# First layer's differences spread over four points, attention's loads and groups moved, two sums of the second layer behind other products, the last block's sums in another order with one on POOL

## The chip, the core and the metric

The kernel runs on one core of a Trainium2 chip. Its engines work side by side and meet by semaphores: TensorE (PE, with its weight loads PEld), VectorE (DVE), ScalarE (ACT), GpSimd (POOL) and SyncE (SP), whose queue issues all the DMAs here. Each engine takes its instructions in the order of the program. The metric is the time of one execution on the device in microseconds, the median of several runs.

## What is computed

Attention in chunks of 32 queries, each over 8 memory slots and a window of 56 keys, and on its result two feed-forward layers, all in fp32:

```
scores = scale * q_c @ k_full.T ; a = softmax(scores) ; out[:, :, chunk] = a @ v_full
x = out.transpose(0, 2, 1, 3).reshape(B * S, H * D)          # 3072 x 512
h = x @ w_in ;  g = relu(h) ** 2            ; x = g @ w_out  # layer 0, d_ff 2048
h = x @ w_in ;  g = h * tanh(log1p(exp(h))) ; x = g @ w_out  # layer 1
```

## The kernel before

The tokens are cut into three blocks (`sb`) of 1024, the hidden dimension into eight parts of 256 (`NQ`). One step is one part of one block of one layer; there are 48, steps 0 to 23 for layer 0 (blocks 0 to 2) and 24 to 47 for layer 1 (blocks 3 to 5 in the code's count). Every fp32 operand is held as a rounded high part and a rest, and a product is made of three matmul passes.

The first matmul of a layer uses a scheme of seven products in place of eight (`PRODUCTS`: P1 to P7, on blocks B11, B21, B12, B22 of x and on the differences T1 = B12 - B11, T2 = B22 - T1, T3 = B22 - B12, T4 = B21 - T2). DVE adds the products up through u1, u2, u3 to c22, c21, c12; P7 may start only when u2 has been read out of its bank, P4 only after u3, P3 only after c22. `gate` applies the activation, and `split_g` (a cast on ACT, a subtraction on POOL) makes the two parts of g. The second matmul belongs to the step before: in layer 0 it is eight `unit`s of six matmuls, unit n for output half t = n // 4 and quarter d = n % 4, summed into `y` by DVE (for the first part of a block it is ACT that copies into y, L547); in layer 1 it is seven `product2`s of six matmuls (`PRODUCTS2`), summed by DVE into tiles m (L558), again by an ACT copy for the first part (L581). When a block is done, the m tiles are combined by the seven additions of `SUMS`, and four of them are stored as the block's output.

`step` writes out the order by hand. Between groups of matmuls it calls `rest()`, which counts points 0 to 14 of a step: it issues the waiting stores (`flush`, in the order of `later`), then the weight loads of that point (`stream_w`), then what was put there by `at(step, point, ...)`. In steps 1 to 24 the points come after P1 (0), P6 (1), P5 (2), units 0 and 1 (3, 4), P2 (5), P7 (6), units 2 to 4 (7 to 9), P4 (10), P3 (11), units 5 to 7 (12 to 14). In steps 25 to 47 they come after P1 (0), P6 (1), product 0 (2), P5 (3), product 1 (4), P2 (5), product 2 (6), P7 (7), products 3 and 4 (8, 9), P4 (10), P3 (11), products 5 and 6 (12, 13).

Put beside the matmuls in this way are the decoding and splitting of the weights (`plan_w`: rebias A/a, decode D/d, sums S/s, round R/r, split L/l), the attention of blocks 1 and 2 (`plan_attention`, groups p = 4 to 7 in steps 0 to 6 and p = 8 to 11 from step 9 on: scores, softmax, exps, normalize, transposes, values, `copy_x`, `sums_x` on POOL, `store_x`), the load and split of the next block's x (`load_x` at points 0 to 6, `split_x` from point 4 of the block's last step), and in layer 1 the loads ahead for the next block. Attention's later groups keep q and p in the tile xt0, k in at0, v and the staged result in at1; the next block's xt use the same tiles.

The differences of a finished block of layer 0 are made in `sums_y`, called at the end of steps 8, 16 and 24: three stores of y, four DVE subtractions into tiles of their own, four stores. The tiles y0 and y1 are taken anew for each block, and in layer 1 for four of the m tiles; a new tile waits for all readers of the old one. In the last step (47) and after it, DVE makes the remaining sums and the additions of the last four units (L603, `last_unit`).

## Time and profile before

| | us |
|---|---|
| median of 3 runs (1128.75, 1129.05, 1133.09) | 1129.05 |
| the profiled execution | 1126.08 |
| its span, first to last instruction | 1124.2 |
| PE / DVE / ACT / POOL busy in it | 1061.5 / 898.6 / 561.6 / 430.5 |
| DMA, mean share of 16 engines | 0.81 |

A busy share is a mean over stages that differ: steps 0 to 15 hold attention and the decoding of the weights, steps 16 to 24 the rest of layer 0, steps 25 to 47 layer 1. PE's matmuls are pipelined, so its busy time holds overlaps; the time from the first matmul of P1 in one step to that in the next is what is called a step's time here. The granted clock is given as a share of 2.4 GHz: 1.00 is the upper of two levels, 0.50 the lower.

### The profile page before, as it was taken

How to read it: one execution, taken by the hardware profiler on the slowest of the kernel's cores; microseconds unless marked ns; L12 is line 12 of the kernel's file. 1: busy time of each engine (PE TensorE's matmuls, PEld its weight loads, DVE VectorE, ACT ScalarE, POOL GpSimd, SP SyncE). 2: the span in 40 equal slices, each digit the busy share in tenths (PEclk: the TensorE clock that was granted, in tenths of full speed). 3: DMA queues.
4: the chain of work that ended last, by engine and by line, in shares of the span. 5: the costliest groups of instructions: out<-in, count | busy, mean ns of one | idle time of the engine just before them, and what ended most of it. 6: DMA issues, size and time to landing. Idle time of an engine off the chain costs nothing.

```text
span 1124.2 us, 19766 instructions
## 1 busy us (share of the span) xinstructions
PE 1061.5 (94%) x7478; PEld 872.3 (78%) x7478; DVE 898.6 (80%) x1170; ACT 561.6 (50%) x879; POOL 430.5 (38%) x327
## 2 busy tenths in 40 slices
PE   5779999897799999999999999999999999999997
PEld 5758787785677887888888878888878888778885
DVE  5686889969756766578999767988888888978888
ACT  2458555546544554647656555443354444444331
POOL 1215233232223333223322244546454554545552
PEclk9998999999989999999999999999999999999999
DMA  9556867777989898969999968989979889797441
GB/s 354 216 186 269 308 228 275 259 265 268 369 316 319 306 333 298 336 237 381 374 345 328 361 225 292 316 312 324 401 247 319 308 307 371 272 315 227 158 155 75
DMA packets 192125, 324.94 MB, mean 289 GB/s; under 512 B 13344, under 2 KB 151072, under 8 KB 188192
## 3 DMA queue, kind: packets, MB, share of 16 engines
q1 hardware_dynamic: 192032, 323.69, 80.9%
q8 instruction: 60, 0.98, 0.3%
q14 instruction: 33, 0.27, 0.1%
HBM read 231.62 MB, written 92.01 MB: 288 GB/s over the span
## 4 chain that ended last, share of the span: by engine, by line
PE 65%; DVE 14%; DMA 6%; issue 4%; ACT 3%; POOL 1%; SPq 0%; DVEq 0%; ACTq 0%; POOLq 0%
PE banks L480 29%; PE banks L535 16%; PE banks L570 15%; DVE m L558 3%; PE banks L416 1%; PE banks L346 1%; DVE r L521 1%; DMA w_d<-hi 1%; DMA w2s<-w_d 1%; DVE y L549 1%; DMA w1s<-w_d 1%; DVE ty L628 1%; DVE val L157 1%; DVE val L158 1%; DVE val L154 1%
## 5 line engine op out<-in xcount | busy, mean ns | idle before, releaser
L480 PE MATMUL banks<-x,w1s 128*128 128x512 f32 x2016 | 502.2, 396 | 19.1 <-DVE u L763 7.3
L494 POOL TENSOR_TENSOR g<-r,g 128x512 fp32r<-128x512 f32 x206 | 289.6, 1412 | 523.1 <-ACT g L493 434.6
L480 PEld LDWEIGHTS banks<-x,w1s 128*128 128x128 f32 x2016 | 382.3, 191 | 104.4 <-DVE u L763 9.0
L535 PE MATMUL banks<-g,w2s 128*128 128x512 f32 x1152 | 279.7, 394 | 6.9 <-DVE y L549 6.7
L535 PEld LDWEIGHTS banks<-g,w2s 128*128 128x128 f32 x1152 | 216.7, 190 | 55.7 <-DVE y L549 8.4
L570 PE MATMUL banks<-g,w2s 128*128 128x512 f32 x966 | 239.0, 390 | 1.2 <-DVE m L558 0.6
L570 PEld LDWEIGHTS banks<-g,w2s 128*128 128x128 f32 x966 | 180.6, 188 | 41.9 <-DVE m L558 2.3
L558 DVE TENSOR_TENSOR m<-banks,m 128x1024 f32<-128x1024 f32 x144 | 173.3, 1218 | 30.5 <-PE banks L570 27.5
L493 ACT CAST g<-r 128x512 fp32r<-128x512 f32 x206 | 127.0, 621 | 31.0 <-DVE r L521 23.7
L549 DVE TENSOR_TENSOR y<-banks,y 128x512 f32<-128x512 f32 x168 | 111.4, 682 | 25.7 <-PE banks L535 25.4
L494 POOL TENSOR_TENSOR g<-more,g 128x512 fp32r<-128x512 f32 x55 | 81.8, 1492 | 77.8 <-ACT g L493 63.2
L499 ACT ACTIVATE r<-r 128x512 f32<-128x512 f32 x72 | 45.4, 631 | 69.5 <-DVE r L771 46.1
L503 ACT ACTIVATE r<-r 128x512 f32<-128x512 f32 x48 | 30.3, 632 | 75.8 <-DVE r L765 38.4
L213 ACT CAST hi<-val 128x1024 fp32r<-128x1024 f32 (+1 forms) x32 | 30.4, 951 | 71.4 <-DVE val L158 42.3
L500 ACT ACTIVATE r<-r 128x512 f32<-128x512 f32 x96 | 60.7, 633 | 3.1
L154 DVE TENSOR_SCALAR val<-val 128x512 f32<-128x512 f32 x64 | 36.7, 573 | 24.4 <-ACT val L147 24.4
L346 PE MATMUL banks<-k,q 64*32 64x64 f32 x1536 | 39.4, 255 | 16.8 <-DMA k<-k_dram 10.1
L346 PEld LDWEIGHTS banks<-k,q 64*32 64x32 f32 x1536 | 33.4, 125 | 21.5 <-issue 18.2
L158 DVE SCALAR_TENSOR_TENSOR val<-raw,val 128x512 uint32<-128x512 uint32 x64 | 47.3, 738 | 2.2
L735 ACT COPY u<-banks 128x512 f32<-128x512 f32 x48 | 27.9, 581 | 41.1 <-PE banks L480 41.0
L386 POOL TENSOR_TENSOR p<-p,sum 128x512 f32<-128x512 f32 x22 | 25.6, 1186 | 57.8 <-DVE sum L383 23.3
L416 PE MATMUL banks<-pt,v 64*64 64x32 f32 x1536 | 35.1, 249 | 11.3 <-ACT pt L404 9.8
(72 smaller groups left out, 991.4 us busy)
## 6 DMA issues: line engine op xcount, KB each, us to landing
w1s<-w_d SPq DMA_DIRECT2D x280, 256.0 KB, 5.5
w2s<-w_d SPq DMA_DIRECT2D x229, 256.0 KB, 5.4
raw<-w_dram SPq DMA_DIRECT2D x64, 512.0 KB, 5.1
w_d<-w1s SPq DMA_DIRECT2D x8, 1792.0 KB, 7.1
x<-xs_d SPq DMA_DIRECT2D x14, 1024.0 KB, 10.7
k<-k_dram SPq DMA_DIRECT2D x24, 512.0 KB, 7.3
v<-v_dram SPq DMA_DIRECT2D x24, 512.0 KB, 8.7
xt<-xt_d SPq DMA_DIRECT2D x21, 512.0 KB, 7.3
```

The source lines that it names most:

```text
L154: nc.vector.tensor_scalar(out=val, in0=val, scalar1=LIMIT, scalar2=-LIMIT * NEGATIVE, op0=ALU.min, op1=ALU.max)
L158: nc.vector.scalar_tensor_tensor(out=vb, in0=low, scalar=29, in1=vb, op0=ALU.logical_shift_right, op1=ALU.bitwise_or)
L346: nc.tensor.matmul(out=s4[32 * c:32 * c + 32, j, hp, :], lhsT=q_t[p][r0:r0 + 64, j, hp, 32 * c:32 * c + 32], rhs=k_t[p][r0:r0 + 64, j, hp, ...
L416: nc.tensor.matmul(out=x_ps[par][64 * h2:64 * h2 + 64, o:o + 32], lhsT=v_t[p][j][r0:r0 + 64, h2, a, c, :], rhs=pt_t[p][r0:r0 + 64, h2, j, ...
L480: nc.tensor.matmul(out=ps, lhsT=w[:, a, f:f + 128], rhs=x[:, xi, c, kk, :], start=start and i == 0, stop=stop and i == len(order) - 1, ski ...
L493: nc.scalar.copy(out=g[:, 0], in_=r)
L494: nc.gpsimd.tensor_tensor(out=g[:, 1], in0=r, in1=g[:, 0].bitcast(FP32), op=ALU.subtract)
L500: nc.scalar.activation(out=r, in_=r, func=ACTF.Square)
L535: nc.tensor.matmul(out=ps, lhsT=w[:, a, blk(f), d % 2 * 128:d % 2 * 128 + 128], rhs=g_t[s, (f, t)][:, c, :], start=i == 0, stop=i == len(o ...
L549: nc.vector.tensor_tensor(out=y, in0=ps, in1=y, op=ALU.add)
L558: engine.tensor_tensor(out=to, in0=in0, in1=in1, op=ALU.add)
L570: nc.tensor.matmul(out=bank(first + d), lhsT=w[:, a, 128 * d:128 * d + 128], rhs=g[:, c, :], start=i == 0, stop=i == 2)
```

## The change

The tile y of a block is used again for the next one instead of being taken anew, and so are the two tiles that hold four of the m tiles. `sums_y` is replaced by `plan_sums`: the stores of B11 and B21 come at points 5 and 9 of the block's last units, the first difference at point 13, the store of B22 and the second difference at point 0 of the next step, the fourth at point 1 and the third at point 3; the fourth is written over B21, the third over B12, and the first two share the tile at1. In attention, the load of v moves from 5 to 8 points behind the group's start; the groups of block 1 follow each other by 24 points instead of 25, those of block 2 start at point 10 of step 8 with a period of 20 instead of point 8 of step 9 with 19, with q and k of the first loaded at points 0 and 1 of step 8. In the weights' plan for steps 8 to 14, r and l move by one point. In layer 1, the sum of B22 and T2 moves from behind product B21 to behind T3, and that of B21 and B11 from behind T3 to behind T1. In the last step the sum of B21 and B11 goes to POOL behind T3, and that of T3 and T2 moves from behind T1 to behind T2.

```diff
--- before.py
+++ after.py
@@ -449,7 +449,7 @@
         nc.vector.tensor_tensor(out=to[1], in0=st, in1=to[0].bitcast(FP32), op=ALU.subtract)
 
 
-    g_t, y_t, m_t = {}, {}, {}
+    g_t, y_t, m_t, m_both = {}, {}, {}, {}
     rings = {"g": 0, "r": 0, "u": 0}
     more = {}
 
@@ -541,7 +541,7 @@
             )
         rest()
         if j == 0 and d == 0:
-            y_t[sb, t] = pool.tile([128, KD, NB], FP32, tag=f"y{t}", name="y")
+            y_t[sb, t] = y_t[sb - 1, t] if sb else pool.tile([128, KD, NB], FP32, tag=f"y{t}", name="y")
         y = y_t[sb, t][:, d]
         if j == 0:
             nc.scalar.copy(out=y, in_=ps)
@@ -576,17 +576,21 @@
             if n < 3:
                 m_t[sb, blk] = pool.tile([128, 2, NB], FP32, tag=spare(sb + 1, n), name="m")
             elif n % 2:
-                both = pool.tile([128, 2, 2, NB], FP32, tag=f"y{n // 5}", name="m")
+                if sb == NSB:
+                    both = pool.tile([128, 2, 2, NB], FP32, tag=f"y{n // 5}", name="m")
+                else:
+                    both = m_both[n]
+                m_both[n] = both
                 m_t[sb, blk], m_t[sb, PRODUCTS2[n + 1][1]] = both[:, 0], both[:, 1]
             nc.scalar.copy(out=m_t[sb, blk], in_=ps)
             return
         m = m_t[sb, blk]
         add(m, ps, m)
 
-    def combine(sb, to, other, store=False):
+    def combine(sb, to, other, store=False, engine=nc.vector):
 
         m = {b: m_t[sb, b] for _, b in PRODUCTS2}
-        add(m[to], m[to], m[other])
+        add(m[to], m[to], m[other], engine)
         if store and (to, other) in SUMS[3:]:
             store_y(sb, *OUTPUTS[to], m[to])
 
@@ -612,22 +616,6 @@
         store_y(sb, i, t, m)
         flush()
 
-    def sums_y(sb):
-        d = xt_d[1][sb]
-        y0, y1 = y_t[sb, 0], y_t[sb, 1]
-        b11, b21, b12, b22 = (i.rearrange("p k s -> p (k s)") for i in (y0[:, 0:2], y0[:, 2:4], y1[:, 0:2], y1[:, 2:4]))
-        nc.sync.dma_start(out=d[:, B11], in_=b11)
-        nc.sync.dma_start(out=d[:, B21], in_=b21)
-        nc.sync.dma_start(out=d[:, B22], in_=b22)
-        if sb < NSB - 1:
-            both = [pool.tile([128, 2, 2 * NB], FP32, tag=f"at{n}", name="ty") for n in range(2)]
-            t = [both[n // 2][:, n % 2] for n in range(4)]
-        else:
-            t = [pool.tile([128, 2 * NB], FP32, tag=("xt0", "xt1", "xt2", "at1")[n], name="ty") for n in range(4)]
-        for n, (t1, t2) in enumerate(((b12, b11), (b22, t[0]), (b22, b12), (b21, t[1]))):
-            nc.vector.tensor_tensor(out=t[n], in0=t1, in1=t2, op=ALU.subtract)
-            later(d[:, T1 + n], t[n])
-
 
     beside = {}
 
@@ -642,7 +630,8 @@
             1: lambda: softmax(p, 0),
             2: lambda: softmax(p, 1),
             3: lambda: (exps(p, 0), exps(p, 1), load_k(p + 1) if (p + 1) % PSB else None),
-            5: lambda: (normalize(p), load_v(p) if p > PSB else None),
+            5: lambda: normalize(p),
+            8: lambda: load_v(p) if p > PSB else None,
             12: lambda: transpose_p(p),
             13: lambda: (copy_pt(p), load_q(p + 1) if (p + 1) % PSB else None),
             16: lambda: values(p),
@@ -651,6 +640,46 @@
             22: lambda: store_x(p),
         }.items():
             at(s, i + n, work)
+
+    def plan_sums(sb):
+
+
+        d = xt_d[1][sb]
+        t = {}
+
+        def blocks():
+            y0, y1 = y_t[sb, 0], y_t[sb, 1]
+            return [i.rearrange("p k s -> p (k s)") for i in (y0[:, 0:2], y0[:, 2:4], y1[:, 0:2], y1[:, 2:4])]
+
+        def minus(n, to, in0, in1):
+            nc.vector.tensor_tensor(out=to, in0=in0, in1=in1, op=ALU.subtract)
+            later(d[:, n], to)
+
+        def first():
+            b11, _, b12, _ = blocks()
+            t["both"] = pool.tile([128, 2, 2 * NB], FP32, tag="at1", name="ty")
+            minus(T1, t["both"][:, 0], b12, b11)
+
+        def second():
+            b22 = blocks()[3]
+            later(d[:, B22], b22)
+            minus(T2, t["both"][:, 1], b22, t["both"][:, 0])
+
+        def fourth():
+            b21 = blocks()[1]
+            minus(T4, b21, b21, t["both"][:, 1])
+
+        def third():
+            _, _, b12, b22 = blocks()
+            minus(T3, b12, b22, b12)
+
+        s = (sb + 1) * NQ
+        at(s, 5, lambda: later(d[:, B11], blocks()[0]))
+        at(s, 9, lambda: later(d[:, B21], blocks()[1]))
+        at(s, 13, first)
+        at(s + 1, 0, second)
+        at(s + 1, 1, fourth)
+        at(s + 1, 3, third)
 
     def plan_w(s, i, e, order, round_, split, val):
 
@@ -718,13 +747,13 @@
             _, sb, j = where(s - 1)
             blk = PRODUCTS2[i][1]
             if s == STEPS - 1:
-                for n in {T2: (0,), T1: (1, 2, 3), T4: (4, 6, 5)}.get(blk, ()):
-                    combine(sb, *SUMS[n])
+                for n in {T3: (6,), T2: (0, 1), T1: (2, 3), T4: (4, 5)}.get(blk, ()):
+                    combine(sb, *SUMS[n], engine=nc.gpsimd if n == 6 else nc.vector)
             elif j == NQ - 1:
                 for n in {T2: (0,), T1: (1,)}.get(blk, ()):
                     combine(sb, *SUMS[n])
             elif sb > NSB and j == 0:
-                for n in {B11: (3,), B22: (4,), B21: (5,), T3: (6,)}.get(blk, ()):
+                for n in {B11: (3,), B22: (4,), T3: (5,), T1: (6,)}.get(blk, ()):
                     combine(sb - 1, *SUMS[n], store=True)
 
         if live:
@@ -786,8 +815,6 @@
             for w in beside.pop((s, i), []):
                 w()
         flush()
-        if prev and where(s - 1)[0] == 0 and where(s - 1)[2] == NQ - 1:
-            sums_y(where(s - 1)[1])
 
     with tc.manual_schedule():
         nc.scalar.preload_act_table_set("natural_log_exp_and_others")
@@ -868,7 +895,7 @@
         seconds = [e for e in order_w if e[0]]
         for n, e in enumerate(seconds):
             if n < NQ - 1:
-                plan_w(NQ + n, 0, e, "Aa|D|d|RS|s|L||||r|l", lambda e, i: round_w2(e, i, "xt2"), split_w2, "val")
+                plan_w(NQ + n, 0, e, "Aa|D|d|RS|s|L|||||r|l", lambda e, i: round_w2(e, i, "xt2"), split_w2, "val")
             else:
                 n -= NQ - 1
                 hi = (["xt0", "xt1"], ["xt2", "at1"])[n % 2]
@@ -879,12 +906,14 @@
 
         for sb in range(NSB - 1):
             p = PSB * (sb + 1)
-            start, first, period = ((0, 4, 25), (NQ + 1, 8, 19))[sb]
+            start, first, period = ((0, 4, 24), (NQ, 10, 20))[sb]
             at(start, 0, lambda p=p: load_q(p))
             if sb:
-                at(start, 0, lambda p=p: load_k(p))
+                at(start, 1, lambda p=p: load_k(p))
             for n in range(PSB):
                 plan_attention(start, first + period * n, p + n)
+        for sb in range(NSB):
+            plan_sums(sb)
 
         for sb in range(1, 2 * NSB):
             s = sb * NQ - 1
```

## Rows read from the trace of the kernel before

**Rows 1.** The page: busy us, share of the span and instructions of each engine.
```profile
PE 1061.5 (94%) x7478; PEld 872.3 (78%) x7478; DVE 898.6 (80%) x1170; ACT 561.6 (50%) x879; POOL 430.5 (38%) x327
```

**Rows 2.** Steps 7-10, 17, 25, 26, 33: from:to us; PE, PEld, DVE, ACT, POOL; clock; DMA.
```profile
239.34:264.87 25.53, 21.59 (x91) 16.59 (x90) 16.38 (x23) 12.61 (x19) 5.58 (x4) 1.00 1.03 377
264.87:288.82 23.95, 21.50 (x92) 16.54 (x90) 19.47 (x30) 13.64 (x20) 5.80 (x4) 1.00 0.72 236
288.82:324.82 36.00, 28.06 (x235) 22.41 (x234) 23.41 (x34) 17.76 (x30) 6.79 (x5) 0.86 1.02 379
324.82:354.23 29.41, 28.23 (x371) 23.36 (x370) 17.49 (x28) 16.63 (x28) 11.38 (x11) 0.94 0.84 289
...
494.12:514.52 20.40, 20.40 (x91) 16.89 (x90) 16.92 (x27) 12.04 (x21) 3.75 (x4) 1.00 0.94 329
...
657.77:678.52 20.75, 19.63 (x86) 15.61 (x84) 14.32 (x15) 12.53 (x18) 10.69 (x7) 1.00 0.76 267
678.52:697.57 19.05, 19.05 (x85) 15.74 (x84) 13.54 (x16) 8.03 (x13) 8.11 (x6) 1.00 0.74 264
812.83:835.00 22.17, 19.64 (x85) 15.61 (x84) 19.53 (x18) 12.20 (x18) 11.55 (x8) 1.00 0.64 215
```

**Rows 3.** PE's groups, steps 7 and 8: busy, mean ns; idle before, what ended it.
```profile
L535 PE MATMUL banks<-g,w2s 128*128 128x512 f32 x97 | 24.2, 396 | 3.7 <-DVE y L549 3.6
L480 PE MATMUL banks<-x,w1s 128*128 128x512 f32 x85 | 21.0, 394 | 2.7 <-DVE u L763 1.4 <-DVE u L744 1.2 <-ACT u L735 0.2
```

**Rows 4.** The same view of steps 9 and 10.
```profile
L480 PE MATMUL banks<-x,w1s 128*128 128x512 f32 x84 | 21.7, 407 | 3.1 <-DVE u L744 3.1
L346 PE MATMUL banks<-k,q 64*32 64x64 f32 x256 | 7.5, 250 | 6.0 <-DMA k<-k_dram 3.1 <-issue 2.9
```

**Rows 5.** As rows 2: two of the four low-clock stretches, and the sum of four.
```profile
308.83:319.07 10.24, 8.52 (x119) 7.12 (x108) 3.65 (x5) 1.63 (x2) 0.20 (x1) 0.50 1.04 380
349.79:353.21 3.42, 3.42 (x10) 2.73 (x9) 1.13 (x2) 1.07 (x2) 1.58 (x2) 0.50 0.72 237
sum 27.31, PE 24.77 PEld 20.84 DVE 11.37 ACT 10.85 POOL 9.84; mean PE 6.19 PEld 5.21 DVE 2.84 ACT 2.71 POOL 2.46
```

**Rows 6.** The chain of waits in steps 6 to 9: start us, us, what.
```profile
238.24 8.18 DMA xt_d<-stage
246.43 5.09 DMA xt<-xt_d
...
300.95 7.55 DMA k<-k_dram
```

**Rows 7.** DVE's timeline, end of step 8: start us, us, engine, line, operation, tiles.
```profile
291.38 2.19 DVE L628 TENSOR_TENSOR ty<-y 128x1024 f32<-128x1024 f32 x1
```

**Rows 8.** DVE's timeline in the tail.
```profile
1105.70 5.21 DVE L558 TENSOR_TENSOR m<-m 128x1024 f32<-128x1024 f32 x3
...
1112.08 3.50 DVE L558 TENSOR_TENSOR m<-m 128x1024 f32<-128x1024 f32 x3
1115.49 4.61 DVE L558 TENSOR_TENSOR m<-banks,m 128x1024 f32<-128x1024 f32 x4
```

**Rows 9.** PE's timeline in steps 13 and 14, with idle time before.
```profile
412.62 0.81 PE L346 MATMUL banks<-k,q 64*32 64x64 f32 x43 [0.99 <-ACT stage L428]
439.44 0.30 PE L416 MATMUL banks<-pt,v 64*64 64x32 f32 x2 [1.07 <-ACT pt L404]
```

**Rows 10.** The page: one of the costliest groups, columns as rows 3.
```profile
L549 DVE TENSOR_TENSOR y<-banks,y 128x512 f32<-128x512 f32 x168 | 111.4, 682 | 25.7 <-PE banks L535 25.4
```

**Rows 11.** The page: DMA issues, KB each, median us from issue to landing.
```profile
v<-v_dram SPq DMA_DIRECT2D x24, 512.0 KB, 8.7
```

**Rows 12.** DVE's timeline in step 33.
```profile
822.80 5.67 DVE L558 TENSOR_TENSOR m<-m 128x1024 f32<-128x1024 f32 x3
```

**Rows 13.** PE's timeline in the tail.
```profile
1105.72 11.04 PE L603 MATMUL banks<-g,w2s 128*128 128x512 f32 x48
```

**Rows 14.** POOL's timeline in step 47.
```profile
1100.62 1.29 POOL L494 TENSOR_TENSOR g<-r,g 128x512 fp32r<-128x512 f32 x1 [1.66 <-ACT g L493]
```

## Prediction

> **What bounds the kernel now.** I read the page's engine line first, then the busy times step by step, then TensorE's idle time by line, and last the chain of waits. TensorE (PE) is busy for 94% of the span and VectorE (DVE) for 80% [rows 1], so the matmul stream is the bound and only its holes can be won. The step table says where they are [rows 2]. Step 17 takes 20.40 us with PE busy throughout, which is the floor of a first-layer step (90 matmuls of 0.227 us); step 26 takes 19.05, the floor of a second-layer step. Against these, step 7 takes 25.53, step 8 23.95, step 9 36.00, step 10 29.41, step 25 20.75, step 33 22.17 (step 41 repeats it). PE stands idle 3.7 + 2.7 = 6.4 us in steps 7 and 8, every time for a DVE result (y, u) [rows 3]. In steps 9 and 10 it is idle 3.1 us for DVE's u and 6.0 us ahead of attention's score matmuls, 3.1 of that for the load of k and 2.9 with no releaser, in a stretch where the DMA engines are full (share 1.02) [rows 2, 4]. Around these holes the granted clock is 0.50, the lower of its two levels, for 10.24 and 3.42 us [rows 5]; at half clock half of the time is lost, 6.8 us.
>
> The chain of waits ties these together: store of attention's staged result (8.18 us to landing), load of xt (5.09), split on ScalarE (ACT) and DVE, DVE in arrears through step 8, then the four differences, then k's load (7.55), then scores [rows 6]. DVE's first difference takes 2.19 us beside POOL [rows 7], where the same shape alone takes 3.50 / 3 = 1.17 [rows 8].
>
> All terms are taken against the profiled execution, 1126.08 us, of which 1124.2 are the span. The median shown, 1129.05, is 2.97 longer, and I add that at the end.
>
> **The change part by part.**
>
> *a. Attention of the second block of tokens, steps 0 to 6.* Period 24 for 25, so its four groups come 0, 1, 2 and 3 points earlier; loads of v stay 8 points ahead of the values matmuls instead of 11. Nothing is added. DVE has the same work in front of the same releases, so what it gives back at one product it takes at the next. I take 0; the move of a queue by up to 3 points (1.4 us each) between a matmul and its reader can go either way, which I bound by a wait of each of the two kinds seen in the later block, 0.99 and 1.07 [rows 9]: -2 to +2.
>
> *b. The same block's end, steps 6 to 8.* The last group's values matmuls move from point 5 of step 6 to point 2, and its store from point 11 to point 8. On SP's queue the store now goes past three points of weight traffic, none of which waits for it. Today the store is issued at 238.24, lands 8.18 later at 246.4, and the xt load starts there at once [rows 6], so the load waits for the store and nothing else. The values matmuls pass P5, units 0 and 1 and P2, four groups of six matmuls at 1.36 us, so ACT's copies, POOL's sums and the store can come 5.4 sooner; it would land near 241. The xt load then waits only for its own place in the queue, behind a weight load at the start of step 7 (239.34 [rows 2]): about 241.5, 4.9 us earlier. DVE then starts its splits 4.9 us earlier. The 6.4 us of PE idle [rows 3] come after that point and all wait for DVE; I take 4.5 of them, bounds 2 (only the first, 1.4 for u L763, and a little) and 6.4 (all).
>
> *c. Sums and attention around steps 8 to 10.* Removed: a burst of four DVE subtractions at the end of step 8 and SP's wait for each of their results, behind which the loads of q and k stood. Added: the first at point 13 of step 8, the others at points 0, 1 and 3 of step 9, the last two in place in y; three stores of y at points 5, 9 and 0; q and k loaded at points 0 and 1 of step 8, scores at its point 10. Same instructions, same bytes. k's wait of 3.1 goes: k is issued nine points, some 12 us, before its use against 7.55 to landing [rows 6]. For DVE I count from the end of P4 in step 8, with 0.68 for a half-size instruction [rows 10] and 1.2 to 1.5 for a difference (between 1.17 alone and 2.19, nearer the first, since POOL is busy for 5.8 of 23.95 us in step 8 [rows 2]): two softmax stages of two 2.8, c12 0.7, three y sums 2.0, first difference 1.2, row sums 1.8, second difference 1.5, decode (three) 1.9, fourth 1.5, u2 0.7, and 3.1 of waits for scores, P3 and unit 5, which are fixed by PE: 17.2 us. PE reaches P7 of step 9 after scores, P3, units 5 to 7, P1, P6, P5, units 0 and 1, P2: 16.4. So u2 still stops PE, for 0.8 instead of 3.1. By the same count u3 (decode, sums, third difference 1.5, split) stops it for 0.7. New waits: v's load at point 3 of step 9 needs the tile at1, so SP stands there until the second difference is stored and read by the fourth; behind it stand w1 and w2 for a later step. v takes 8.7 [rows 11] and would be late by 0.9. ACT's copies of the next block's y (units 2 and 4 of step 9) wait for the stores of the fourth and third difference; behind them stand the gate of c21 and the bank of unit 5, four groups or 5.4 us later, so 0. The missing-releaser idle I leave at 1.2 of 2.9 and the half-clock loss at 1.7 of 6.8, as in step 10 today. The two steps move 23.95 x 236 + 36.00 x 379 = 19.3 MB; at the 379 GB/s of step 9 [rows 2] that needs 50.9 us, against my 51 for both, so I add 1.5 for DMA. Left over: 0.8 + 0.7 + 0.9 + 1.2 + 1.7 + 1.5 = 6.8 of 3.1 + 6.0 + 6.8 = 15.9. Gain 9; bounds 4 (only k's wait and a fifth of the clock) and 14. The four second-layer weight points moved by one (r and l of the split) carry l past c21, which costs nothing where DVE waits for scores there.
>
> *d. Last group of that block, steps 13 and 14.* Period 20 for 19: PE's waits of 0.99 for ACT's copy out of the bank and 1.07 for pt [rows 9] get one point and another neighbourhood. Gain 1.5, 0 to 2. The load of v, now six points behind the previous store instead of two, frees SP, which nobody waits for.
>
> *e. Step 25.* Before, the four differences of the third block hold back u2 and a g. Now one of them lies in step 24 and one behind u2. Step 25 is 20.75 - 19.05 = 1.7 over its floor [rows 2]. Gain 1.3, 0 to 1.7.
>
> *f. Steps 33 and 41.* In step 33 three sums stand on DVE ahead of u3, 5.67 us in all [rows 12], and PE waits for it. The change puts one of them behind the product T3, that is behind u3 and c22 on DVE. The first two lie beside POOL's splits; the one that leaves is the last and takes the short time, so u3 comes 5.67 / 3 = 1.9 us sooner at most, and 1.15 if it runs alone as in the tail [rows 8]. I take 1.15 for each of two steps, 2.3. The sum that goes behind T1 falls into DVE's wait for ACT. Bounds 0 and twice the whole excess, 6.2.
>
> *g. Tail.* Chain: DVE's sums. After T1's product three sums take 5.21, after T4's three take 3.50, and the four last adds 4.61 end it at 1120.1, while PE's last units begin at 1105.72 and take 11.04, to 1116.8 [rows 8, 13]. One sum (1.17) leaves DVE for POOL; another goes ahead of c21. POOL needs twice the 1.29 of a half-size subtraction [rows 14], 2.6, an estimate, and has room before 1105. c21 comes 1.2 to 2.2 later, since a sum beside POOL takes up to twice as long [rows 7]; then PE's last units end some 0.7 later, at 1117.5, and the last add can't end before 1118.8. DVE by itself would end at 1118.9 plus POOL's disturbance. Gain 0.6; bounds -0.5 and 1.3. The Trainium skill's page "SBUF — State Buffer", section "Who interferes with whom", speaks against this move: a DVE instruction with two SBUF inputs and a GpSimd instruction that reads SBUF shut each other out for their whole length. By that rule the sum ahead of c21 would wait out all of POOL's sum, c21 would come 3.9 later, and the tail would lose 0.5 instead of gaining 0.6. The trace's 2.19 beside POOL against 1.17 agrees with mutual delay.
>
> Sum: 0 + 4.5 + 9 + 1.5 + 1.3 + 2.3 + 0.6 = 19.2. 1126.08 - 19.2 = 1106.9, and with 2.97 for the median 1109.9: 1110. The low ends together give 3.6 (1125.5), the high ends 33.7 (1095).
>
> **Rivals.** *The wait moves, not the work.* Steps 8 and 9 now hold two attention stages more on a DVE that is busy 19.5 of 23.95 us in step 8 [rows 2]; adding softmax (2.8) and a difference (1.2) gives 23.5 of some 24. If it stays in arrears, u2 and u3 stop PE for as long as today and only k's wait goes: b 2, c 4, the rest 4.2, in all 10: 1119. For it: every PE idle in steps 7 and 8 names DVE. Against: DVE's splits start earlier and its total does not grow.
>
> *Hidden anyway.* If steps 8 to 10 are held by the DMA engines (share 1.02), removing waits in front of them frees nothing, and only e to g remain, 4.2: 1125. Against: step 8 has a share of 0.72 to spare.
>
> *The clock falls, slower.* Scores are many small matmuls; after a hole in front of them PE got the lower level for 10.24 us in step 9, but not each time: all low stretches of the kernel together are 27.31 us [rows 5], a loss of 13.7. Were each of the eight score groups to draw 10.24 us at half clock because DVE's new order leaves a hole beside them, the loss would be 8 x 5.12 + 3.4 = 44.4, 30.7 more than now, against gains other than the clock's of 19.2 - 5.1 = 14.1: 1129 + 16.6 = 1146. It decides from five of the eight groups on; today two do so.
>
> **How the numbers follow.** Forecast (1103 to 1116) 0.58; wait moves (1119) 0.22; hidden (1125) 0.10; clock (1146) 0.06; better than all that, near the high ends (1098) 0.04. Below 1101 and above 1122 lie about 0.2, so the range is 1101 to 1122. About 0.5%, 5.6 us, is what a measurement of this kernel can tell from no change. Faster: 0.58 + 0.22 + 0.04 and a little of the third, 0.86; same 0.08; slower 0.06.
>
> **What would show it.** Right: no wait for k before scores in step 8 and none of 8 us for xt in step 7; steps 7 to 10 together at about 101 instead of 114.9; step 25 at 19.4; steps 33 and 41 at 21.0; last add ending some 0.6 earlier behind PE's last units. Wrong: PE idle for u in steps 8 and 9 above 2 us; clock 0.50 after the moved scores; SP or ACT standing at the new stores.

## The result, and the profile after

The changed kernel takes 1112.54 us in the median of four runs (1110.46 to 1115.69) against 1128.9 before: ratio 0.9851, 95% interval 0.9816 to 0.9886. Run once more beside the first experiments it took 1112.11 (0.9868, 0.9838 to 0.9898). The forecast was 1110, 1101 to 1122. That the sum came so near hides large misses in four of its terms, which the traces show.

The page's engine line, busy us and share of the span (1113.9 us), against [rows 1]:

```profile
PE 1059.9 (95%) x7478; PEld 871.3 (78%) x7478; DVE 904.5 (81%) x1169; ACT 561.4 (50%) x879; POOL 436.1 (39%) x328
```

The same steps as [rows 2], then 12, 13, 14 and the tail (columns as there; the tail runs from the first matmul of step 47 to the end of the span):

```profile
237.97:261.83 23.86, 21.32 (x91) 16.61 (x90) 16.19 (x23) 12.42 (x18) 5.60 (x4) 1.00 1.03 381
261.83:288.72 26.89, 24.40 (x235) 19.02 (x234) 22.74 (x35) 16.50 (x25) 7.04 (x5) 1.00 0.90 313
288.72:315.93 27.21, 24.22 (x228) 19.79 (x226) 17.86 (x28) 12.87 (x23) 7.80 (x5) 1.00 1.03 380
315.93:345.89 29.96, 27.36 (x243) 22.64 (x242) 19.83 (x34) 17.79 (x30) 11.20 (x11) 0.89 0.87 315
...
370.56:402.35 31.79, 28.68 (x372) 23.38 (x370) 19.94 (x33) 16.90 (x29) 11.92 (x11) 0.95 0.95 336
402.35:425.89 23.54, 23.54 (x227) 19.60 (x226) 17.78 (x29) 11.83 (x20) 6.92 (x6) 1.00 0.77 258
425.89:446.29 20.40, 20.40 (x91) 16.89 (x90) 13.81 (x23) 9.86 (x16) 7.44 (x7) 1.00 0.85 282
650.32:669.36 19.04, 19.04 (x86) 15.77 (x84) 13.75 (x15) 12.75 (x18) 11.03 (x7) 1.00 0.87 287
803.81:824.83 21.02, 19.63 (x85) 15.61 (x84) 19.50 (x18) 12.19 (x18) 11.53 (x8) 1.00 0.65 215
1075.43:1113.90 38.47, 30.67 (x133) 24.44 (x131) 32.51 (x28) 7.76 (x13) 15.41 (x9) 1.00 0.14 55
```

Attention's groups stand in other steps now, so steps 8 to 14 can't be set against each other one by one; their sum can. Steps 0 to 6 together take 177.25 us against 177.91 before, steps 7 to 14 208.32 against 213.59, steps 16 and 18 are 0.8 shorter, step 25 by 1.7, steps 33 and 41 by 1.15 and 1.14, the tail is 0.94 longer. That is 0.7 + 5.3 + 0.8 + 1.7 + 2.3 - 0.9 = 9.9, and step 0 begins 0.7 sooner: 10.6, which some hundredths in the other steps bring to the 10.3 of the two spans; the two profiled executions (1126.08 and 1115.69) show 10.4. The medians differ by 16.4. The profiled execution of before lies 2.8 under its median and that of after 3.2 over its own.

Four traces hold the change's steps 0 to 46 unaltered: this one, that of the second run, and those of the first two experiments below, which touch only the tail. They show how far executions of the same steps differ (us):

| | the change | second run | tail as before | POOL's sum kept |
|---|---|---|---|---|
| start of step 47 (before the change: 1086.68) | 1075.43 | 1074.93 | 1071.60 | 1071.72 |
| steps 0 to 6 | 177.25 | 177.28 | 174.81 | 176.24 |
| steps 7 to 14 | 208.32 | 207.35 | 206.34 | 205.03 |
| step 12 | 31.79 | 30.55 | 29.95 | 29.12 |
| wait for u2 in step 9 | 2.58 | 2.79 | 2.46 | 2.41 |
| wait of the scores in step 10 | 2.60 | 2.25 | 1.22 | 0.97 |

So the gain up to step 47 is 11.3 to 15.1 us. The last two traces come to step 47 some 3.8 us sooner than the change's own, all of it in steps 0 to 14; that is about what its profiled execution lies over its median. For the 2.8 on the side of before there is no second trace, and they stay open. A difference of 3 us between two single traces in steps 7 to 14, or of 2.7 in step 12, is no sign of an edit. (For the second run I had expected step 12 within 1 us of 31.8 if the order of the work makes it, and under 29 if a chance fall of the clock does; it took 30.55, which is neither.)

The holes that are left between steps 7 and 12: first PE's groups in steps 7 and 8 (as [rows 3]), then its timeline of steps 9 to 12 (start, us, what; in brackets the idle time before and what ended it):

```profile
L535 PE MATMUL banks<-g,w2s 128*128 128x512 f32 x97 | 24.2, 396 | 3.7 <-DVE y L549 3.6
L480 PE MATMUL banks<-x,w1s 128*128 128x512 f32 x84 | 20.8, 395 | 1.4 <-DVE u L773 1.2 <-ACT u L764 0.2
```

```profile
299.62 1.67 PE L480 MATMUL banks<-x,w1s 128*128 128x512 f32 x6 [2.58 <-DVE u L773]
309.44 2.35 PE L416 MATMUL banks<-pt,v 64*64 64x32 f32 x128 [0.42 <-DMA v<-v_dram]
320.05 0.33 PE L346 MATMUL banks<-k,q 64*32 64x64 f32 x8 [2.60 <-ACT stage L428]
...
380.27 3.01 PE L480 MATMUL banks<-x,w1s 128*128 128x512 f32 x12 [1.85 <-ACT u L764]
384.36 0.30 PE L416 MATMUL banks<-pt,v 64*64 64x32 f32 x2 [1.07 <-ACT pt L404]
```

The wait for k and the idle time without releaser [rows 4] are gone. But u2 still stops PE for 2.58 where 3.1 stood, scores wait 2.60 for a bank that ACT has to empty (L428), and step 12 has two holes that were not there. Behind the scores of step 10 and the holes of step 12 the clock is at the lower level again, as it was in [rows 5]:

```profile
321.70:328.53 6.83, 6.83 (x73) 5.60 (x65) 4.20 (x8) 1.95 (x4) 2.08 (x3) 0.50 0.38 130
386.55:389.97 3.42, 3.42 (x31) 2.77 (x25) 1.23 (x2) 2.04 (x5) 1.32 (x2) 0.50 0.91 302
```

### The profile page after: what moved, and what is told of

The parts are those of the page before. It is cut to its first block, busy times and chain, and to the rows that moved or that the text cites. A ratio compares the mean times of both kernels' runs of the same rounds, so it can differ in the third digit from the quotient of the medians.

```text
span 1113.9 us, 19775 instructions
## 1 busy us (share of the span) xinstructions
PE 1059.9 (95%) x7478; PEld 871.3 (78%) x7478; DVE 904.5 (81%) x1169; ACT 561.4 (50%) x879; POOL 436.1 (39%) x328
## 4 chain that ended last, share of the span: by engine, by line
PE 59%; DVE 8%; DMA 3%; issue 2%; ACT 1%; SPq 0%; DVEq 0%; POOL 0%; ACTq 0%
PE banks L480 29%; PE banks L570 17%; PE banks L535 13%; DVE m L558 3%; DMA w_d<-hi 2%; DVE r L521 1%; DMA w_d<-val 1%; DMA w1s<-w_d 0%; DVE more L521 0%; PE banks L346 0%; DVE y L549 0%; PE banks L416 0%; DVE u L773 0%; DVE val L220 0%; DVE val L157 0%
## 5 line engine op out<-in xcount | busy, mean ns | idle before, releaser
L535 PEld LDWEIGHTS banks<-g,w2s 128*128 128x128 f32 x1152 | 216.8, 190 | 55.1 <-DVE y L549 8.3
L558 DVE TENSOR_TENSOR m<-banks,m 128x1024 f32<-128x1024 f32 x144 | 173.3, 1217 | 30.3 <-PE banks L570 27.1
L154 DVE TENSOR_SCALAR val<-val 128x512 f32<-128x512 f32 x64 | 39.2, 613 | 29.5 <-ACT val L147 29.5
L220 DVE TENSOR_TENSOR val<-val,hi 128x1024 f32<-128x1024 f32 (+1 forms) x32 | 36.3, 1136 | 17.4 <-ACT hi L213 17.1
L386 POOL TENSOR_TENSOR p<-p,sum 128x512 f32<-128x512 f32 x22 | 27.1, 1250 | 54.2 <-DVE sum L383 28.7
L147 ACT ACTIVATE val<-raw 128x512 f32<-128x512 f32 x64 | 40.3, 666 | 14.0 <-DMA w_d<-val 14.0
```

The costliest lines, as they stand in the source:

```text
L147: nc.scalar.activation(out=val, in_=high.bitcast(FP32), func=ACTF.Prelu, scale=REBIAS, alpha=NEGATIVE)
L154: nc.vector.tensor_scalar(out=val, in0=val, scalar1=LIMIT, scalar2=-LIMIT * NEGATIVE, op0=ALU.min, op1=ALU.max)
L535: nc.tensor.matmul(out=ps, lhsT=w[:, a, blk(f), d % 2 * 128:d % 2 * 128 + 128], rhs=g_t[s, (f, t)][:, c, :], start=i == 0, stop=i == len(o ...
L558: engine.tensor_tensor(out=to, in0=in0, in1=in1, op=ALU.add)
```

## The experiments

My theory after the two traces: the steps of the sum name the right places, and what failed has three causes. The xt load goes out 6.5 us sooner but lands late, because two stores of weights stand right ahead of it; u2 is late because DVE meets l, which waits for ACT behind a store, ahead of the softmax; and in the tail POOL's sum and DVE's shut each other out. Rivals: DVE has simply too much to do in steps 7 to 9 (then moving stores gives nothing); the four differences need not have been spread, since removing their stores from SP's queue is enough; and the gain is attention's new places, not the sums.

**The tail as before.**

```diff
-for n in {T3: (6,), T2: (0, 1), T1: (2, 3), T4: (4, 5)}.get(blk, ()):
-    combine(sb, *SUMS[n], engine=nc.gpsimd if n == 6 else nc.vector)
+for n in {T2: (0,), T1: (1, 2, 3), T4: (4, 6, 5)}.get(blk, ()):
+    combine(sb, *SUMS[n])
```

> The changed kernel with the last step's sums in their old order, all on DVE. Theory of the prediction (DVE's sums end the kernel, one less is a gain): the stretch from step 47 to the end 0.6 us longer than in the changed kernel. Rival (the sum on POOL shuts DVE's sum ahead of c21 out, c21 comes 2.1 us late and PE's last units wait for it): 0.9 us shorter than the changed kernel, 37.5 us, no idle time of PE before the last units.

1112.01 us, ratio 0.986 (0.9827 to 0.9893), beside 1112.11 of the change: a few tenths can't be told by the times. The traces can. From step 47 to the end it took 37.54 us, as before, against 38.47 and 39.10 in the two traces of the change (in the second the clock fell in PE's hole). PE's last units run without a break:

```profile
1090.64 11.04 PE L607 MATMUL banks<-g,w2s 128*128 128x512 f32 x48
```

In the change they are broken twice:

```profile
1094.47 0.61 PE L607 MATMUL banks<-g,w2s 128*128 128x512 f32 x2
1097.11 0.96 PE L607 MATMUL banks<-g,w2s 128*128 128x512 f32 x3 [2.02 <-ACT g L493]
1098.47 10.05 PE L607 MATMUL banks<-g,w2s 128*128 128x512 f32 x43 [0.40 <-POOL g L494]
```

DVE's and POOL's timelines of the change say why:

```profile
1090.49 4.61 DVE L558 TENSOR_TENSOR m<-m 128x1024 f32<-128x1024 f32 x2
1095.02 0.68 DVE L800 TENSOR_TENSOR more<-banks,u 128x512 f32<-128x512 f32 x1
...
1090.63 3.39 POOL L558 TENSOR_TENSOR m<-m 128x1024 f32<-128x1024 f32 x1
```

DVE's two sums should take 2 x 1.17; the first does, the second ends 1.1 us after POOL's, which ends at 1094.02. So c21 (L800) comes 2.1 later than DVE alone would bring it, and with it g of the last units. Against the kernel with the old tail, where one sum less stands ahead of it, c21 comes 3.3 later: 19.6 us into step 47 for 16.3.

**POOL's sum kept, the sum of T3 and T2 back behind T1.**

```diff
-for n in {T3: (6,), T2: (0, 1), T1: (2, 3), T4: (4, 5)}.get(blk, ()):
+for n in {T3: (6,), T2: (0,), T1: (1, 2, 3), T4: (4, 5)}.get(blk, ()):
```

> The changed kernel with the sum of T3 and T2 of the last step back behind T1, and the sum of B21 and B11 still on POOL behind T3. Theory (what costs in the tail is the DVE sum that stands between POOL's sum and c21, and not POOL's sum itself): c21 comes where it came before, PE's last units have no idle time, DVE has one sum less behind T1 and T4, and the stretch from step 47 to the end is 36.3 to 36.9 us, against 38.5 to 39.1 in the changed kernel and 37.5 with the old order. Rival (any sum on POOL costs as much as it saves): 37.5 or more.

1110.30 us, 0.9841 (0.9813 to 0.9869). The tail takes 36.59, that is 0.95 less than before and 1.9 less than the change. DVE's timeline, POOL's and PE's:

```profile
1086.78 1.27 DVE L558 TENSOR_TENSOR m<-m 128x1024 f32<-128x1024 f32 x1
1087.97 0.68 DVE L800 TENSOR_TENSOR more<-banks,u 128x512 f32<-128x512 f32 x1
1090.75 5.40 DVE L558 TENSOR_TENSOR m<-m 128x1024 f32<-128x1024 f32 x3
...
1086.92 3.40 POOL L558 TENSOR_TENSOR m<-m 128x1024 f32<-128x1024 f32 x1
...
1090.77 11.04 PE L607 MATMUL banks<-g,w2s 128*128 128x512 f32 x48
```

c21, which reads one operand from a bank, takes its 0.68 in the midst of POOL's sum, and PE has no hole. Giving a sum to POOL pays; what didn't was the other sum that was put beside it.

**Two stores of weights put off in step 7**, w1 of the last part and w2 of the one before it, from their places ahead of the xt load to point 7:

```diff
-            later((w1_d, w2_d)[kind][0][j], w.bitcast(FP32))
+            store = lambda: later((w1_d, w2_d)[kind][0][j], w.bitcast(FP32))
+            if e in ((0, NQ - 1, 0), (0, NQ - 2, 1)):
+                at(NQ - 1, 7, store)
+            else:
+                store()
```

> The changed kernel with two stores of weights (1792 and 1024 KB, issued at 235.4 and 238.3 us just ahead of the loads of xt) put off to point 7 of step 7, behind those loads. Theory (xt starts when predicted, but takes 8.5 us to land instead of 5.1 because these stores fill the DMA engines): xt lands in some 5 us, ACT's first split starts 3 us sooner, and the 5.0 us of PE idle in steps 7 and 8 fall to 2 to 3, so steps 7 and 8 come out at 48 instead of 50.8. Rival (DVE's own work in steps 7 and 8 makes the idle time, whenever xt lands): the same idle time within 1 us.

1111.59 us, 0.9846 (0.9812 to 0.988). First the change itself, SP's issues and ACT's first split:

```profile
235.37 0.33 SPq L131 DMA_DIRECT2D w_d<-w1s  x1
238.29 0.33 SPq L131 DMA_DIRECT2D w_d<-w2s  x1
238.71 1.21 SPq L247 DMA_DIRECT2D w1s<-w_d  x1
239.97 2.93 SPq L261 DMA_DIRECT2D xt<-xt_d  x2
...
248.48 1.05 ACT L275 CAST x<-xt 128x1024 fp32r<-128x1024 f32 x1 [7.05 <-DMA xt<-xt_d]
```

Then the kernel with the stores put off, in which lines from 207 on stand four further down: ACT's first split, and step 7 whole (columns as the steps above).

```profile
242.15 1.05 ACT L279 CAST x<-xt 128x1024 fp32r<-128x1024 f32 x1 [0.49 <-DMA xt<-xt_d]
```

```profile
238.20:259.04 20.84, 20.78 (x92) 16.74 (x90) 16.18 (x23) 12.56 (x18) 5.60 (x4) 1.00 0.99 337
```

Step 7 loses 3.0 of its 23.86 us (it took 23.86 to 24.63 in the four traces of the change's steps) and stands near the floor of 20.40. So it was the load and not DVE's work that held step 7; the rival of a DVE with too much to do falls there. The edit did two things for the load: SP issues it 2.4 us sooner, counted from the start of step 7, and it lands 4.4 us after its issue where it took 8.5. Step 8 does not depend on it: its time stays (26.92), and so do PE's 1.1 us for y and 1.2 for u. Nor is DVE simply full there. Ahead of the sum for which PE waits 1.1, DVE itself stands 1.24 us for ACT's cast of x, in the change and with the stores put off alike; that cast comes behind a gate for which ACT had waited for DVE. DVE's timeline of the change:

```profile
264.99 1.47 DVE L277 TENSOR_TENSOR x<-xt,x 128x1024 fp32r<-128x1024 f32 x1 [1.24 <-ACT x L275]
```

The kernel as a whole gains only 0.5, within the intervals, though steps 7 to 14 take 201.94 in the trace, 3.1 to 6.4 less than in the four traces of the change's steps: u2's wait in step 9 grew to 3.38, and the tail, which this kernel has unchanged, took 39.41.

**r and l of the split at their old points.**

```diff
-plan_w(NQ + n, 0, e, "Aa|D|d|RS|s|L|||||r|l", ...)
+plan_w(NQ + n, 0, e, "Aa|D|d|RS|s|L||||r|l", ...)
```

> The changed kernel with r and l of the weights' plan for steps 8 to 14 back at points 9 and 10. Theory of the prediction (the move costs and gives nothing): no difference in steps 8 to 15 beyond 1 us. Rival (l one point later stores the tile val one point later, and ACT's rebias at the next step's start waits for that store: 14.0 us in the changed kernel, 8.3 before): ACT's wait for w_d<-val falls to some 8 us, step 12 loses its 1.85 us of PE idle for u, and steps 8 to 15 together come 2 to 5 us shorter.

1116.03 us, 0.989 (0.9858 to 0.9922), 4 us more than the change; the two intervals overlap. Step 12 took 28.99, hardly less than the shortest of the four traces (29.12). But ACT's decoding waits less for the store of val (12.2 to 15.5 us in those four traces). That view, the waits, of the change and then of this kernel (us in total, times, longest):

```profile
ACT val L147 <- DMA w_d<-val: 14.0, 5, 4.7
```

```profile
ACT val L147 <- DMA w_d<-val: 6.2, 3, 2.5
```

Against that, u2's wait in step 9 is 3.16 for 2.41 to 2.79 and step 9 takes 29.40. In the traces both kernels need the same for steps 7 to 14 (207.5 and 205.03 to 208.32). So moving r and l is worth some 4 us by the medians, which neither of my two expectations had, and it has a price in ACT's wait for val that my prediction didn't have. By which mechanism it is worth them isn't settled.

**The high part's tile apart.** l waits for ACT's r, and r waits for the store of the high part before it, since both use one tile. In four of the seven weights of steps 8 to 14 the second half gets another:

```diff
-... lambda e, i: round_w2(e, i, "xt2"), ...
+... lambda e, i, n=n: round_w2(e, i, "xt1" if i and n in (0, 3, 4, 6) else "xt2"), ...
```

> The changed kernel with a tile of its own (xt1, free at that time) for the second rounded half of the weights in steps 8, 11, 12 and 14, so that ACT's rounding r does not wait until the first half's store has landed. Theory (PE's 2.6 us of waiting for u2 in step 9, where 0.8 was predicted, come from l: it stands on DVE ahead of the softmax and waits for r, which waits 1.7 us for that store): l comes about 2 us sooner in step 8, u2's wait in step 9 falls to 0.5 to 1.2 us, ACT's waits for w_d<-hi fall from 14 to under 9 us; 2 to 4 us shorter in all. Rival (DVE's own work between P4 of step 8 and u2 is longer than counted, by POOL's work beside it): u2's wait stays above 2 us.

1111.48 us, 0.987 (0.9841 to 0.9898), on a chip where before took 1126.96. In the change DVE's l (L220) stands ahead of the softmax's row maximum (L369):

```profile
284.39 1.22 DVE L220 TENSOR_TENSOR val<-val,hi 128x1024 f32<-128x1024 f32 x1 [2.38 <-ACT hi L213]
285.54 0.68 DVE L369 TENSOR_REDUCE mx<-banks 128x8 f32<-128x512 f32 x1
```

With the tile apart, DVE's timeline and then PE's at u2:

```profile
281.98 1.52 DVE L220 TENSOR_TENSOR val<-val,hi 128x1024 f32<-128x1024 f32 x1 [0.57 <-ACT hi L213]
283.43 0.68 DVE L369 TENSOR_REDUCE mx<-banks 128x8 f32<-128x512 f32 x1
```

```profile
297.52 1.65 PE L480 MATMUL banks<-x,w1s 128*128 128x512 f32 x6 [1.07 <-DVE u L773]
```

DVE is 1.5 us further on in its step (2.1 by the clock, since step 8 itself begins 0.6 sooner), u2's wait falls from 2.58 to 1.07 (2.41 to 2.79 in the four traces), and ACT's waits for the stores of the high part fall from 14.2 in all to 5.8. That confirms the chain store, r, l, softmax, u2. The 2 to 4 us that I expected from it for the whole kernel do not show in its time here.

**The third difference sooner**, right behind the fourth, so that the store of it, for which ACT's copy of y waits, goes out sooner:

```diff
-        at(s + 1, 1, fourth)
-        at(s + 1, 3, third)
+        at(s + 1, 1, fourth, third)
```

> The changed kernel with the third difference made at point 1 of the step behind the fourth, instead of at point 3. Theory (in step 9 ACT's copy of unit 4's y waits 2 us for the store of the third difference, with it the copy out of the bank that the next scores need, which stand 2.6 us in step 10): ACT's wait for the store of y falls to 0, the scores' wait for ACT in step 10 falls by about 2 us, and PE's wait for u2 in step 9 grows from 2.6 by 1.2, the length of one difference. In all about 1 us shorter. Rival (the scores wait for the gates and the weights' rounding ahead of that copy on ACT): the scores' wait stays within 0.7 us and the kernel is 1 us longer.

1115.21 us, 0.989 (0.9855 to 0.9924): slower than the change by 3, with intervals that overlap, where I had expected 1 us less. In the change ACT stands 2.36 us for that store, then for another, and only then copies attention's result out of the bank that the next scores need (L428):

```profile
312.44 0.59 ACT L547 COPY y<-banks 128x512 f32<-128x512 f32 x1 [2.36 <-DMA xt_d<-y]
314.62 1.05 ACT L213 CAST hi<-val 128x1024 fp32r<-128x1024 f32 x1 [1.59 <-DMA w_d<-hi]
...
319.42 1.06 ACT L428 COPY stage<-banks 128x512 f32<-128x512 f32 x2
```

Here both ACT's wait for y and PE's 2.60 at the scores are gone, and step 10 takes 24.20 for 29.96 (27.1 at least in the four traces). But the difference now stands ahead of u2, and that wait grows:

```profile
302.03 2.93 PE L480 MATMUL banks<-x,w1s 128*128 128x512 f32 x6 [4.17 <-DVE u L772]
```

So the wait was rightly named, and moving the difference trades it for u2's: steps 9 and 10 take 55.1 together, in the four traces 55.0 to 57.2. That trade is no loss in the trace (steps 7 to 14: 205.36). What is longer lies behind: steps 15 to 46 take 631.9 against 629.1 to 629.4. Step 25, where the edit puts the third block's difference ahead of u2, waits for u2 again and takes 20.13 for 19.04. Step 16 has a new wait for y of 0.9 and takes 22.15 for 20.4 to 20.6; whether the edit makes it isn't shown.

**The four differences together at point 0.**

```diff
-        at(s, 13, first)
-        at(s + 1, 0, second)
-        at(s + 1, 1, fourth)
-        at(s + 1, 3, third)
+        at(s + 1, 0, first, second, fourth, third)
```

> The changed kernel with all four differences at point 0 of the next step, as a burst like before, in the new tiles. Theory of the prediction (spreading them over points 13, 0, 1 and 3 is part of the gain): PE's wait for u2 in step 9 grows from 2.6 to about 5 us, step 25 gets back its 1.7 us over 19.05, the kernel is 3 to 5 us longer. Rival (what counts is that SP's queue and the tiles let k and q through sooner, wherever the sums stand): u2's wait within 1 us of 2.6, step 25 within 0.5 of 19.05, time within 1.5 us.

1114.90 us, 0.9887 (0.9858 to 0.9917), 2.8 over the change's median, again with intervals that overlap. Step 25 is back at 20.75, with the two waits that it had before (PE's timeline):

```profile
658.09 1.66 PE L480 MATMUL banks<-x,w1s 128*128 128x512 f32 x6 [0.53 <-DVE u L770]
661.68 1.66 PE L570 MATMUL banks<-g,w2s 128*128 128x512 f32 x6 [0.58 <-ACT m L585]
```

Steps 9 and 10, where u2's wait is 3.65, take 54.5 together, not more than the 55.0 to 57.2 of the four traces, and steps 7 to 14 take 205.1. So the spread is worth 1.7 in step 25; another 1 by the medians isn't shown. The gain around step 8 doesn't hang on it.

**Attention's groups, v and k at their old points**, the rest of the change kept:

```diff
-            5: lambda: normalize(p),
-            8: lambda: load_v(p) if p > PSB else None,
+            5: lambda: (normalize(p), load_v(p) if p > PSB else None),
...
-            start, first, period = ((0, 4, 24), (NQ, 10, 20))[sb]
+            start, first, period = ((0, 4, 25), (NQ + 1, 8, 19))[sb]
...
-                at(start, 1, lambda p=p: load_k(p))
+                at(start, 0, lambda p=p: load_k(p))
```

> The changed kernel with attention's loads, starts and periods as before the change (25 and 19 points, second group at point 8 of step 9, q and k loaded at points 0 there, v 5 points behind the start); sums and tail stay. Theory of the prediction (most of the gain of steps 7 to 14 comes from k's load being early and from the earlier store of the staged result): step 7 back at 25.5, PE waits for k in step 9 again by 2 us or more, steps 7 to 14 together 5 us or more longer than the changed kernel's 208. Rival (taking the stores of the differences out of SP's queue is what frees k): k's wait under 0.5 us and steps 7 to 14 within 2 us of 208.

1120.30 us, 0.993 (0.9908 to 0.9952): with the rest of the change in place, attention's places are worth one half of its gain. Steps 7 and 14:

```profile
238.05:263.49 25.44, 21.58 (x91) 16.60 (x90) 16.37 (x23) 12.59 (x19) 5.58 (x4) 1.00 1.03 375
...
423.27:451.03 27.76, 25.46 (x228) 20.74 (x227) 15.00 (x25) 13.44 (x22) 9.77 (x10) 0.94 0.85 286
```

Steps 0 to 6 take 177.61 against 174.8 to 177.3, so of block 1's part of the move no gain can be told from the spread; step 7 is back at before's 25.5, and steps 7 to 14 at 212.98, 4.7 to 8.0 above the four traces. Neither expectation held in full. The wait for k is absent here too, which the rival said: before, SP stood 4.8 us at the stores of the differences and issued k at 300.5, here at 291.7, and the new load points weren't needed for that. But the time did not come within 2 us of 208. What comes back are PE's idle times without releaser in front of scores, 2.13 in step 9 and 3.18 in step 10 (2.9 in all before, none in steps 7 to 14 of the four traces), and ACT's copy of u1 late by 1.54 in step 9 and 2.30 in step 14, each time behind ACT's wait for the store of val. That wait is 23.2 us in all here, 8.3 before. So part of this half may be a price of the moved r and l that is larger beside attention's old places.

**Together.** The tail's repair and the put-off stores, and then the tile apart as well (the edits shown above, nothing else).

> The changed kernel with the tail of tail_pool and the two stores of stores_put_off together. Both act in different steps, so they should add: steps 7 and 8 at 47.8 as in stores_put_off, step 47 to the end at 36.6 as in tail_pool, a profiled span of 1106 to 1108 and a median of 1106 to 1110 us. If the time that steps 7 and 8 give up is paid back in steps 9 to 14 (waits for DMA and ACT there), the median stays at tail_pool's 1110.

> best1 with the separate tile of hi_apart as well. If u2's wait in step 9 is l's wait for the store, 2 to 4 us below best1: a median of 1103 to 1107 us. If it is not, within 1.5 us of best1.

1109.33 us, 0.9839 (0.981 to 0.9869), and 1105.19 (1104.49 to 1107.49), 0.9815 (0.9786 to 0.9845). By its time the first can't be told from the tail's repair alone (1110.30). The second beats both kernels, and is 6 us below the 1111.48 that the tile apart alone took on the same chip. Its steps 7 to 10:

```profile
236.38:257.23 20.85, 20.78 (x92) 16.74 (x91) 16.18 (x23) 12.55 (x18) 5.58 (x4) 1.00 0.98 337
257.23:284.12 26.89, 24.42 (x236) 19.02 (x234) 24.16 (x37) 17.51 (x27) 7.20 (x6) 1.00 1.03 396
284.12:310.06 25.94, 24.14 (x227) 19.71 (x226) 16.91 (x26) 12.12 (x22) 7.65 (x5) 1.00 1.03 395
310.06:337.59 27.53, 24.53 (x243) 20.10 (x242) 18.39 (x33) 15.80 (x27) 10.08 (x11) 1.00 0.88 320
```

The granted clock is 1.00 in all four, where each of the four traces of the change's steps has a stretch at the lower level in steps 9 to 10 (0.89 in step 10 of the change), and steps 7 to 14 take 201.0 for 205.03 to 208.32.

## Why the prediction was right, and where it was not

*a, 0: right as far as can be told.* Steps 0 to 6 moved by 0.7 in this trace and by up to 3.1 in the others; undoing the move there moves them by 0.4.

*b, 4.5: the mechanism half right, the term too big.* The load was issued at 239.97, 2.0 us into step 7; the 241.5 of the working is 2.2 us into it. The step that failed is "the xt load then waits only for its own place in the queue", with 5.09 us to landing taken over from [rows 6]: two stores of 1792 and 1024 KB now went out 4.6 and 1.7 us ahead of it, and it landed after 8.5. Of the 6.4 us of idle time only the 1.4 for u went. With the stores put off, step 7 gives the 3.0 more. The 2.3 of waits for y and u in step 8 stay even then, so they hang on the order of the work there and not on the load; DVE's own idle time for ACT's cast (1.24) stands in front of the first of them. (Nor does all of the 6.4 wait for DVE: 0.2 of it in [rows 3] names ACT.)

*c, 9 and d, 1.5: too big.* Steps 7 to 14 gave 5.3 in this trace and up to 8.6 in the others, where b, c and d had 15. With b's 1.4 taken off, 3.9 to 7.2 are left for c and d, near the low end of c's own bounds of 4 to 14. Right: k's 3.1 went. Better than worked out: no idle time without releaser was left (1.2), u3 did not stop PE in step 9 (0.7), and v stopped it for 0.42 (0.9). Wrong in three places. For u2, 0.8 was left by a count of DVE's work, and 2.58 was measured: the count had no l, of which the prediction says that it "costs nothing where DVE waits for scores there". It waits for ACT's r, and that for a store (the 2.38 at L220). For ACT's copies of y, "5.4 us later, so 0" counted c21's gate and unit 5 behind them but not the copy of attention's result out of its bank, which came behind them at 319.42 and stopped PE at the next scores for 2.60 (0.97 to 2.60 in the four traces), with 6.83 us at half clock after it. And for d, the 0.99 and 1.07 of [rows 9] did go (steps 13 and 14 take 23.54 and 20.40), but 1.85 and 1.07 came up in step 12 in their place (0.75 to 2.21 and 1.03 to 1.07 in the four traces), in this trace with 3.42 at half clock. In part this is the rival "the wait moves, not the work", which gave 1119 and had 0.22; what it lacked is that the low clock in steps 7 to 14 got less as well: 13.7 us before, 3.4 to 10.2 in the four traces.

*e, 1.3: right, 1.7 measured.* Step 25 is at the floor of 19.05, and with the differences together it is back at 20.75.

*f, 2.3: right, 2.29 measured.* Steps 33 and 41 give 1.15 and 1.14, the value for a sum that runs alone [rows 8].

*g, +0.6: wrong, -0.94 measured.* The failed step is the price of the sum ahead of c21 beside POOL: "a sum beside POOL takes up to twice as long", 1.2 to 2.2 later. The sum waited until POOL's was done, and c21 came 3.3 later. POOL's sum took 3.39 us and not the estimate of 2.6; 1.1 of that lies beside DVE's first sum, which had begun 0.14 ahead of it, and what POOL takes alone no run shows. The end followed as worked out: the last add ends 1.3 behind PE's last unit (1109.8 and 1108.5). The rule of the Trainium skill's page "SBUF — State Buffer", section "Who interferes with whom", by which the two instructions shut each other out for their whole length, gave -0.5 and so the right sign. The trace agrees with it: 3.39 of POOL, and DVE's sum done 1.1 after that. It agrees also for an instruction with one input in SBUF, which by the same section isn't held up: c21 took 0.68 in the midst of POOL's sum.

*Hidden anyway* is refuted by the last kernel, whose steps 7 to 14 are 12.6 us shorter than before with the same bytes, and *the clock falls* by the time (it gave 1146) and by the traces: 27.3 us at the lower level before, and up to step 47 17.1 to 27.3 in the four traces (23.9 in the change's own).

Of the prediction's own signs of being wrong, all three came: PE idle for u in steps 8 and 9 for 3.8 us in place of 2 at most, the clock at 0.50 after moved scores, ACT standing 2.36 at a new store. Steps 7 to 10 took 107.9 and not about 101. (The low and the high ends of the parts add up to 3.5 and 33.6, not 3.6 and 33.7; the times given for them stay.)

The sum of 19.2 was 8.9 too big against the 10.3 of the two traces, and about 5 too big against the two traces with other tails (14.1 with the change's tail put in). The forecast of 1110 still came within 2.5 of the median because the medians differ by 6 more than the two traces do. That nearness is in good part luck; the signs of steps 25, 33 and 41 are not.

## What to carry to other kernels

When a load is moved up in a queue, its landing time changes with what stands right ahead of it: look at the bytes issued in the few microseconds before its new place, large stores above all, and move those too. When you count an engine's work up to a deadline, count every instruction in its order, with what each of them waits for on the other engines; an instruction that is short by itself (l, 1.2 us) can bring another engine's wait along. Give the slower engine a piece of work only beside instructions of the faster one that don't meet it; here those were the additions with one operand in a bank. And before you read an edit's worth from one trace, look how far traces of the same steps differ: here 3.3 us over eight steps.

## What the hardware showed that I had not expected

Two adds of 128 x 1024 on DVE and POOL that overlap are done one after the other: 3.39 us of POOL, and DVE's, begun in between, ends 1.1 after it, where alone it takes 1.17. DVE's addition of 128 x 512 with one operand in a bank kept its 0.68 in the midst of such a POOL sum.

A hole in front of PE need not cost its length only: behind 2.60 us for the scores' bank the granted clock stood at 0.50 for 6.83 us, some 3.4 us lost on top. Yet no such stretch followed the 2.58 for u2 in step 9. In the four traces of the same steps the wait for u2 (2.41 to 2.79) was followed by 3.41 us at 0.50 twice and by none twice, with the shorter waits the ones that were followed. So its length doesn't tell it beforehand. In the kernel with all three repairs the lower level shows in steps 1 to 5 alone (6.8 us at 81.4, 3.4 at 136.0, 3.4 at 207.6) and not from step 6 to the end of the last matmul.
